# A chunk-selecting attention with an RMS-normed SwiGLU behind it: another recorded engine order, chunk bounds kept as maximum and spread, and the first block's FFN in halves of 128 tokens

## The chip, the cores and the metric

The kernel runs on one core of a Trainium2 chip. Its engines each work through a queue of their own: PE (TensorE, matrix products), DVE (VectorE), ACT (ScalarE), POOL (GpSimd) and SP, which here only starts transfers. The metric is the device time of one execution in microseconds (us); of several executions the median is given.

## The reference

Four sequences of 768 tokens with 8 heads of 64 go through an attention that looks at 6 chunks of 32 keys for each query, and the result goes through a gated FFN:

```python
k_min = np.min(k_chunks, axis=3); k_max = np.max(k_chunks, axis=3)
ub = np.sum(np.maximum(q[:, :, :, None, :] * k_min[:, :, None, :, :],
                       q[:, :, :, None, :] * k_max[:, :, None, :, :]), axis=-1)
ub = np.where(causal, ub, -1e9)
top_chunks = np.argsort(ub, axis=-1)[..., -6:]          # of 24 chunks
scores = np.where(sel & (pos[:, None] >= pos[None, :]), 0.125 * q @ k.T, -1e9)
attn = softmax(scores) @ v                               # (4, 8, 768, 64)
x  = attn.transpose(0, 2, 1, 3).reshape(3072, 512)
xn = x / np.sqrt(np.mean(x * x, -1) + 1e-6) * rms_g
g, val = xn @ w_gate, xn @ w_val                         # 512 -> 1536
out = (g * sigmoid(g) * val) @ w_out                     # 1536 -> 512, float32
```

All inputs are float32 in device memory. `ub` is an upper bound of a query's scores in a chunk.

## The kernel before, in words

The 3072 tokens are cut in 12 blocks of 256 (`ORDER`, line 340): block i is part m of sequence b. For each block and each of its two groups of four heads (`job`, line 605) the work is:

- **Loads** (`load_qk`, `load_v`, lines 423 to 457). k and q come on SP's queue (for block 0 half of them on ACT's, two k loads and two q loads on each, k ahead of q), v and the weights `wg`, `wv`, `wo`, each in three parts, on POOL's. A load of k or q in blocks 0 to 2 ("packed") holds both head groups, later ones hold one.
- **Chunk bounds.** DVE transposes k and q (`turn`, line 628), takes the minimum and maximum of each chunk (`ext0`, `ext1`, line 646) into `kx`, and DVE or POOL forms the spread maximum minus minimum (`dk`, line 652). `bd0` and `bd1` (m = 0) or `KX` (m > 0) spread these into the matrices `BO` and `BD`. With min, and relu(q) (line 725, DVE or POOL), the bound is q·min + relu(q)·(max − min), which PE sums in `upper` (lines 506 to 539).
- **Selection** (`pick`, line 481): DVE turns the bounds (`ubn`), bars a chunk that lies after the query (`bar`), finds the six largest (`top`), compares (`mk`) and turns the mask back (`mt`, `swap`).
- **Attention.** PE multiplies scores and adds the mask times `chunkrow` (lines 751, 762), ACT exponentiates (`exp`, line 801), POOL cuts the triangle (`tri`, line 771), PE multiplies by v with a column of ones (`values`, line 827), DVE divides (`rden`, `norm`, lines 842, 846).
- **Norm** (line 853): a square on ACT, the root on POOL, a scaling (`scale`) on DVE or ACT, a turn on PE (blocks 0 to 3) or by transfers on SP (the others), and for blocks 0 to 3 a multiplication by the gain into `xsT` (line 919).
- **FFN** (line 928): a group is 8 or 16 products with `wg` or `wv` into one of four PSUM buffers `F` (512 columns). Each gate group goes through a tanh on ACT (line 958) and `tg` on DVE (line 962), each value group through a copy on ACT (line 970) and `hh` on POOL (line 973), or `hh` on DVE (line 966). The 12 parts of the hidden layer are then multiplied by `wo` (`project`, line 998), halved into `osb` and stored. In blocks 0 and 1 (`SPLIT`) the first third of the hidden layer is done by 128 tokens at a time (four hidden parts a group, 16 products of 128 columns), so that the FFN can begin when half the block's attention is done; the rest by 256 tokens (two hidden parts a group, 8 products of 256 columns). Either way a group writes 512 columns, and the block has 12 gate and value groups.

What sets the order: nothing is decided at run time. The source calls `plan.op(...)` for each step in program order, and `Plan.run` (line 227) then emits them in the order of the table `STEPS` (lines 47 to 153): a positive entry is 8 times the operation's number plus the engine that does it (steps of `flex`, line 378, can be done by several engines), a negative entry is a run of idle-filling PE products into an `F` buffer (`keep_busy`, line 1063). `SLOTS` (line 156) says which buffer of its pool each step takes. Each engine works through its steps strictly in this order; a step that waits holds up all behind it on its engine. The search that made the table isn't part of the kernel.

The planner's costs beside the operations (for example `0.585, 0.67` in line 646) were used by that search alone; they do nothing when the kernel runs.

Of the kernel before, what the change touches and what calls it, by code (L numbers as in the profile page):

```python
# [8 lines left out]
FP32 = mybir.dt.float32  # L9
BF16 = mybir.dt.bfloat16  # L10
ALU = mybir.AluOpType
# [5 lines left out]
MASKED = -30000.0  # L17
NEG = -1.0e30
HUGE = 3.0e38
# [14 lines left out]
class Plan:  # L34
# [8 lines left out]
    SHARES = ("qx", "scale", "relu", "bd0", "bd1", "dk", "mk")  # L43
# [1053 lines left out]
```

## Time and profile before

| what | value |
|---|---|
| median of 3 runs | 296.39 us (295.38, 296.39, 299.51) |
| the profiled execution's own time | 299.22 us |
| its span, first to last instruction | 297.2 us |
| PE busy | 283.2 us |
| DVE busy | 222.1 us |
| ACT busy | 207.7 us |
| POOL busy | 164.8 us |
| granted TensorE clock, mean | 0.988 |

The profiled execution took 2.0 us more than its span and 2.8 us more than the median. The table counts idle-filling products of line 1066 as busy time of PE, and matmul ends are modelled, so "busy" isn't the same as "useful". The views used below are the page itself, the table of busy time by stretches, the timeline of one engine, groups of instructions by line and shape, the chain that ended last, and the transfers issued in a stretch with their time to landing. Where two times stand at the head of a line of a timeline, they are the start and the duration in us; a bracket gives the idle time before it and what ended it.

### The profile page before, as it was taken

The page shows a single profiled execution, that of the slowest core. Times are in us where ns is not written, and L with a number is a line of the kernel's source. Part 1 is how long each engine was busy: PE and PEld are TensorE (multiplying, and loading weights), DVE is VectorE, ACT ScalarE, POOL GpSimd, SP SyncE. Part 2 cuts the span into 40 slices and gives each one's busy share as a digit, 9 for nine tenths or more (in the row PEclk, how much of TensorE's full clock was granted, in tenths as well). Part 3 has the DMA queues.
Part 4 walks back from the last instruction along what each step waited for, and adds up shares of the span by engine and source line. Part 5 has one row for each costly group of instructions (what it writes and reads, how often), then busy time and mean ns, then how long its engine had stood idle before and what let it go on. Part 6 is the DMA issues. An engine that isn't in the chain of part 4 may idle for free.

```text
span 297.2 us, 11321 instructions
## 1 busy us (share of the span) xinstructions
PE 283.2 (95%) x4667; PEld 214.8 (72%) x4667; DVE 222.1 (75%) x633; ACT 207.7 (70%) x360; POOL 164.8 (55%) x259
## 2 busy tenths in 40 slices
PE   7796998999999999999999999999899999999995
PEld 7544897576867866888776787678668876688773
DVE  4785696899999899998979999978844643447141
ACT  2674786598797986898876797478596777564331
POOL 6985377969889887457593366209141253112510
PEclk9989799999999999999999999999999999999999
DMA  7999996955698877594979455202214001412012
GB/s 188 207 210 207 204 195 114 163 149 65 122 204 145 156 120 117 124 119 103 151 125 152 101 73 99 73 4 73 20 37 109 2 0 37 74 37 71 2 71 71
DMA packets 86387, 31.92 MB, mean 107 GB/s; under 512 B 74817, under 2 KB 81729, under 8 KB 86337
## 3 DMA queue, kind: packets, MB, share of 16 engines
q1 hardware_dynamic: 55776, 22.82, 33.5%
q0 software_dynamic: 29712, 7.87, 26.5%
q8 instruction: 36, 0.59, 0.9%
q10 hardware_dynamic: 848, 0.53, 0.8%
q14 instruction: 15, 0.11, 0.2%
HBM read 28.58 MB, written 6.29 MB: 117 GB/s over the span
## 4 chain that ended last, share of the span: by engine, by line
PE 60%; DVE 19%; DMA 7%; ACT 5%; POOL 4%; issue 3%; ACTq 0%; DVEq 0%
PE F L951 31%; PE F L998 15%; DMA VX<-in_v_dram 6%; PE F L827 5%; PE S L751 4%; DVE kx L646 3%; DVE m L576 2%; DVE tg L962 2%; ACT pt L801 2%; DVE qT L631 2%; PE S L762 2%; DVE mk L582 2%; DVE BD L473 2%; PE F L517 1%; DVE xnat L846 1%
## 5 line engine op out<-in xcount | busy, mean ns | idle before, releaser
L801 ACT ACTIVATE pt<-S 128x1024 bf16<-128x1024 f32 (+3 forms) x104 | 85.6, 861 | 32.7 <-PE S L762 27.6
L973 POOL TENSOR_TENSOR hh<-tg,vs 128x512 bf16<-128x512 bf16 x48 | 56.1, 1176 | 40.2 <-ACT vs L970 20.3
L951 PE MATMUL F<-xsT,wg 128*128 128x256 bf16 (+1 forms) x608 | 73.4, 268 | 1.9 <-DVE xnat L846 0.9
L962 DVE SCALAR_TENSOR_TENSOR tg<-th,F 128x512 bf16<-128x512 bf16 x72 | 48.1, 677 | 35.1 <-ACT th L958 33.8
L951 PE MATMUL F<-xsT,wv 128*128 128x256 bf16 (+1 forms) x608 | 73.3, 269 | 0.9 <-DVE tg L962 0.7
L998 PE MATMUL F<-wo,hh 128*128 128x512 bf16 (+1 forms) x300 | 68.8, 371 | 0.1
L951 PEld LDWEIGHTS <-wg 128*128 128x128 bf16 x608 | 55.6, 98 | 11.5 <-issue 2.3
L951 PEld LDWEIGHTS <-wv 128*128 128x128 bf16 x608 | 55.5, 98 | 10.4 <-issue 1.7
L771 POOL TENSOR_SCALAR_AFFINE_SELECT pt<-pt 128x512 bf16<-128x512 bf16 x48 | 31.9, 671 | 41.2 <-ACT pt L801 41.0
L958 ACT ACTIVATE th<-F 128x512 bf16<-128x512 f32 x72 | 42.7, 604 | 17.2 <-PE F L951 15.8
L998 PEld LDWEIGHTS <-hh 128*128 128x128 bf16 x300 | 27.9, 98 | 26.1 <-issue 1.2
L970 ACT ACTIVATE vs<-F 128x512 bf16<-128x512 f32 x48 | 28.2, 597 | 10.7 <-PE F L951 8.1
L751 PE MATMUL S<-qb,kb 32*128 32x256 bf16 (+1 forms) x800 | 32.8, 254 | 0.4 <-POOL kx L652 0.4
L646 DVE TENSOR_REDUCE kx<-kT 128x16 f32<-128x512 f32 x48 | 30.9, 669 | 0.0
L827 PE MATMUL F<-VX,pt 128*128 128x65 bf16 x672 | 27.5, 195 | 3.0 <-DMA VX<-in_v_dram 2.6
L827 PEld LDWEIGHTS <-pt 128*128 128x128 bf16 x672 | 25.5, 98 | 6.5 <-issue 2.9
L366 POOL DMA_DIRECT2D VX<-in_v_dram x24 | 22.9, 954 | 0.0
L751 PEld LDWEIGHTS <-kb 32*128 32x128 bf16 x800 | 13.6, 93 | 12.8 <-issue 11.4
L762 PE MATMUL S<-mtd,chunkrow 32*128 32x128 bf16 (+2 forms) x384 | 20.4, 204 | 0.0
L762 PE MATMUL S<-mto,chunkrow 32*128 32x128 bf16 (+2 forms) x384 | 19.8, 203 | 0.0
L846 DVE TENSOR_TENSOR xnat<-F,rden 128x256 bf16<-128x256 f32 x48 | 19.2, 412 | 0.7
L762 PEld LDWEIGHTS <-chunkrow 32*128 32x128 bf16 x768 | 18.6, 94 | 0.9
(72 smaller groups left out, 339.9 us busy)
## 6 DMA issues: line engine op xcount, KB each, us to landing
out_dram<-osb SPq DMA_DIRECT2D x23, 256.0 KB, 2.5
kraw<-in_k_dram SPq DMA_DIRECT2D x72, 64.0 KB, 3.1
qraw<-in_q_dram SPq DMA_DIRECT2D x72, 64.0 KB, 3.0
VX<-in_v_dram POOLq DMA_DIRECT2D x24, 128.0 KB, 5.0
QX<-qT SPq DMA_DIRECT2D x32, 64.0 KB, 2.9
wg<-in_moe_w_gate_dram POOLq DMA_DIRECT2D x3, 512.0 KB, 10.0
wv<-in_moe_w_val_dram POOLq DMA_DIRECT2D x3, 512.0 KB, 14.7
wo<-in_moe_w_out_dram POOLq DMA_DIRECT2D x3, 512.0 KB, 17.1
```

Of the source, the lines that this page charges most:

```text
L646: plan.op(f"ext{n}{J}", "DVE", 0.585, 0.67, lambda n=n, op=op: VE.tensor_reduce(out=at(kx)[:, g, n], in_=at(kT).rearrange("p h (j c x) -> ...
L751: TE.matmul(s[a // 2][:, a % 2, c0:c0 + q1 - q0], kbt[r, t, ks], qbt[r, t, q0:q1], start=(t == 0), stop=(t == 1 and not mask), skip_group_ ...
L762: TE.matmul(o, chunkrow[r, BLK * kg + P * e:BLK * kg + P * (e + 1)], mv, start=False, stop=(d == 1), skip_group_check=True)
L771: GE.affine_select(out=d, in_=d, compare_op=ALU.is_ge, fill=0.0, base=0, pattern=[[0, 4], [1, P]], channel_multiplier=-1)
L801: lambda pt=pt, hs=hs, c0=c0, c1=c1, x=sc[hp]: SE.activation(out=at(pt)[:, hs, c0:c1], in_=at(x)[:, :, c0:c1], func=ACT.Exp, scale=SCALE), ...
L827: TE.matmul(o[:, a, :], p_[:, a, off:off + P], vt[:, e, 4 * g + a, :], start=(kb_ == 0 and a == 0), stop=(kb_ == nkb - 1 and a == 3), skip ...
L951: TE.matmul(at(p_)[:, n * W:(n + 1) * W], w[:, g, ht * P:(ht + 1) * P], at(xT)[:, g, x0:x0 + W], start=(g == 0), stop=(g == NP - 1), skip_ ...
L958: plan.op(f"tanh{U}.{hp}", "ACT", 0.48, 0.6, lambda th=th, gp=gp: SE.activation(out=at(th), in_=at(gp), func=ACT.Tanh, scale=0.5), pri - 0 ...
L962: VE.scalar_tensor_tensor(out=at(tg), in0=at(th), scalar=1.0, in1=at(gp), op0=ALU.add, op1=ALU.mult), pri - 30, reads=[th, gp], writes=[tg ...
L970: plan.op(f"vcopy{U}.{hp}", "ACT", 0.48, 0.6, lambda vs=vs, vp=vp: SE.activation(out=at(vs), in_=at(vp), func=ACT.Copy), pri + 0.1, reads= ...
L973: plan.op(f"hh{U}.{hp}", "POOL", 1.11, 1.16, lambda tg=tg, vs=vs, hh=hh: GE.tensor_tensor(out=at(hh), in0=at(tg), in1=at(vs), op=ALU.mult) ...
L998: TE.matmul(at(op)[:, cs], at(key)[:, o:o + P], wo[:, ht, cs], start=(ht == 0), stop=(ht == NHT - 1), skip_group_check=True)
```

## The change

- **Another table.** `STEPS` and `SLOTS` are new throughout, so every engine has another order, and steps with a choice of engine may sit on another one.
- **Bounds.** `kx` now has three planes: minus the minimum (`negate` in the reduction), the maximum, and the spread. The spread is the sum of the first two. Where DVE does it, it is a `tensor_reduce` over the plane axis in place of a `tensor_tensor`; on POOL it stays a `tensor_tensor`. The bound is now q·max + relu(−q)·(max − min), the same number. `relu` can also be done by ACT.
- **FFN.** `CUT` gives the part of the hidden layer that is done by 128 tokens: all of it in block 0, the first third in block 1 as before.
- **Loads.** Block 0's loads can be on SP or ACT each; readiness of k and q is told by head group, so that a turn waits for its own group's loads; `KX` waits no more for k's buffer; `rmsg` isn't tied behind q.
- `chunkrow` can be made by ACT, and the wide filling products read the identity four times over in place of `chunkrow`.

```diff
-    SHARES = ("qx", "scale", "relu", "bd0", "bd1", "dk", "mk")
+    SHARES = ("qx", "scale", "relu", "bd0", "bd1", "mk")
...
-        67, 228, 233, 3, 131, 27, 249, 244, 50, 260, 281, 34, 58, 9, 276, 265, 19, 99, 115, 139,
+        99, 260, 67, 228, 3, 123, 9, 249, 19, 131, 107, 244, 27, 233, 276, 281, 315, 34, 268, 115,
...
-    buffers("kx", 6, [P, NG, 2, 2, CB], FP32)
+    buffers("kx", 6, [P, 3, NG, 2, CB], FP32)
...
+    CUT = {0: NHT, 1: NHT // 3}
...
-        plan.op("chunkrow", "DVE", 0.8, 0.9, lambda: VE.tensor_scalar(
+        def chunks(eng):
+            if eng is SE:
+                return lambda: SE.activation(out=out, in_=x, func=ACT.Copy, scale=MASKED)
+            return lambda: eng.tensor_scalar(out=out, in0=x, scalar1=MASKED, scalar2=None, op0=ALU.mult)
...
-            eng = ("SP", "ACT")[n % 2] if i == 0 else "SP"
...
+                dma(f"load {nm}{b}{m}{a}{k_}", ("SP", "ACT") if i == 0 else ("SP",), sv, dst, packets, cost,
+                    loads_due(i, nm == "q"), writes=[key + (g,) for g in gs],
...
-                axis=AXXY if packed else AXX, op=op), base + 1, ...
+                axis=AXXY if packed else AXX, op=op, negate=not n), base + 1, ...
...
         def sub(eng):
+            if eng is VE:
+                return lambda: VE.tensor_reduce(
+                    out=at(kx)[:, 2, g], in_=at(kx)[:, 0:2, g].rearrange("p n t c -> p t c n"), axis=AXX, op=ALU.add)
             return lambda: eng.tensor_tensor(
-                out=at(kx)[:, g, 1], in0=at(kx)[:, g, 1], in1=at(kx)[:, g, 0], op=ALU.subtract)
+                out=at(kx)[:, 2, g], in0=at(kx)[:, 1, g], in1=at(kx)[:, 0, g], op=ALU.add)
...
-                    reads=[kx_, bd, kraw] + [kx_ + (x, "d") for x in range(NG)], writes=[bd, bd + (m_,)])
+                    reads=[kx_, bd] + [kx_ + (x, "d") for x in range(NG)], writes=[bd, bd + (m_,)])
...
-                eng.tensor_scalar(out=o, in0=x, scalar1=HUGE, scalar2=0.0, op0=ALU.min, op1=ALU.max)
+                if eng is SE:
+                    SE.activation(out=o, in_=x, func=ACT.Relu, scale=-1.0)
+                else:
+                    eng.tensor_scalar(out=o, in0=x, scalar1=-1.0, scalar2=0.0, op0=ALU.mult, op1=ALU.max)
...
-        cut = NHT // 3 if i in SPLIT else 0
+        cut = CUT.get(i, 0)
...
-    plan.ops[-1].after.append([o for o in plan.ops if o.dma and o.name.startswith("load q00")][-1])
...
-            x = chunkrow[:, 0:512] if wide else ident[:]
-            TE.matmul(store["F"][slot][:, 0:x.shape[1]], ident[:], x, start=True, stop=True)
+            n_ = 4 if wide else 1
+            TE.matmul(store["F"][slot][:, 0:n_ * P].rearrange("p (a b) -> p a b", a=n_), ident[:],
+                      ident[:].unsqueeze(1).to_broadcast([P, n_, P]), start=True, stop=True)
```

What the new table says at the places that the prediction speaks of (before, then after):

| engine | before | after |
|---|---|---|
| SP, first | k, k, q, q of block 0 | q, k, k, q, q of block 0 |
| ACT, first | k, k, q, table load, q | table load, k, k, q |
| POOL's transfers, in order | v0 (both halves), wg0, wg1, wv0, wv1, v1 (both halves), wg2, wv2, wo0, wo1, wo2 | wv0, v0 (first half), wg1, v0 (second), v1 (both halves), wg0, wv1, wg2, wv2, wo0, wo2, wo1 |
| PE, filling products: 128 columns, 512 columns | 85, 26 | 71, 28 |
| `dk`: DVE, POOL | 8, 16 | 13, 11 |
| `relu`: DVE, POOL, ACT | 8, 16, 0 | 2, 17, 5 |
| `chunkrow` | DVE | ACT |
| `scale` of block 2, first half | ACT | DVE, behind block 3's selection |

More of the change, by code (lines that the diff above doesn't have):

```diff
@@ L18 @@
 NEG = -1.0e30
-HUGE = 3.0e38
 class Op:
@@ L333 @@
     wo = sb.tile([P, NHT, DM], BF16, name="wo")
-    BD = {b: sb.tile([P, NG, 2, 2, 32], FP32, name=f"BD{b}") for b in range(B)}
+    BD = {b: sb.tile([P, 2, NG, 2, 32], FP32, name=f"BD{b}") for b in range(B)}
     VX = {(b, m): sb.tile([P, 2, H, D + 1], BF16, name=f"VX{b}{m}") for b in range(B) for m in range(NBLK)}
@@ L360, in due_ffn @@
         return PACE * i
-    def dma(name, eng, src, dst, packets, cost, pri, writes, takes=(), reads=(), behind=()):
-        occ = {"SP": 0.49 if pri < -400 else 0.57, "ACT": 0.46, "POOL": 0.78 if packets < 64 else 1.2}[eng]
-        def start():
-            o.inst = issuer[eng].dma_start(out=dst(), in_=src)
-            for p in fences:
-                tc.add_manual_dep(o.inst.ins, p.inst.ins.name, mybir.DependencyInfo(
-                    mybir.DependencyClass.Sync, mybir.DependencyReason.DATA), reason="order")
-        fences = [p for key in behind for p in plan.wrote[key]]
-        o = plan.op(name, eng, occ, occ, start, pri,
-                    reads=list(reads) + list(behind), writes=writes, takes=takes)
-        o.dma = (packets, cost, eng != "POOL")
-        o.slack = MARGIN if pri > -30 and eng == "SP" else 0.0
-        return o
     def flex(name, alts, pri, **kw):
@@ L381, in flex, with dma, start, go @@
         o.alts = alts
+        return o
+    def dma(name, engs, src, dst, packets, cost, pri, writes, takes=(), reads=(), behind=()):
+        engs = (engs,) if isinstance(engs, str) else engs
+        occ = {"SP": 0.57, "ACT": 0.46, "POOL": 0.78 if packets < 64 else 1.2}
+        def start(eng):
+            def go():
+                o.inst = issuer[eng].dma_start(out=dst(), in_=src)
+                for p in fences:
+                    tc.add_manual_dep(o.inst.ins, p.inst.ins.name, mybir.DependencyInfo(
+                        mybir.DependencyClass.Sync, mybir.DependencyReason.DATA), reason="order")
+            return go
+        fences = [p for key in behind for p in plan.wrote[key]]
+        o = flex(name, {e: (occ[e], occ[e], start(e)) for e in engs}, pri,
+                 reads=list(reads) + list(behind), writes=writes, takes=takes)
+        o.dma = (packets, cost, engs[0] != "POOL")
         return o
@@ L403, in constants @@
             -378, reads=["ident"], writes=["pat"])
-        plan.op("chunkrow", "DVE", 0.8, 0.9, lambda: VE.tensor_scalar(
-            out=chunkrow.rearrange("p (c t) -> p c t", t=CH),
-            in0=pat[:, 0:S // CH].unsqueeze(2).to_broadcast([P, S // CH, CH]),
-            scalar1=MASKED, scalar2=None, op0=ALU.mult), -300, reads=["pat"], writes=["chunkrow"])
+        def chunks(eng):
+            out = chunkrow.rearrange("p (c t) -> p c t", t=CH)
+            x = pat[:, 0:S // CH].unsqueeze(2).to_broadcast([P, S // CH, CH])
+            if eng is SE:
+                return lambda: SE.activation(out=out, in_=x, func=ACT.Copy, scale=MASKED)
+            return lambda: eng.tensor_scalar(out=out, in0=x, scalar1=MASKED, scalar2=None, op0=ALU.mult)
+        flex("chunkrow", {"DVE": (2.2, 2.29, chunks(VE)), "ACT": (0.75, 0.84, chunks(SE))}, -300,
+             reads=["pat"], writes=["chunkrow"])
         for i, (key, t) in enumerate(BD.items()):
@@ L426, in load_qk @@
         first = True
-        for n, a in enumerate((0, 2, 1, 3)):
-            eng = ("SP", "ACT")[n % 2] if i == 0 else "SP"
+        for a in (0, 2, 1, 3):
             rows = slice(32 * a, 32 * (a + 1))
@@ L431, in load_qk @@
                 sv = src[b].rearrange("(g a) (m r j) d -> a m r g (j d)", a=4, m=NBLK, r=32)[a, m]
-                todo = [(sv, lambda rows=rows: at(key)[rows].rearrange("r g j h d -> r g (j h d)"),
-                         4, 0.104 if i == 0 else 0.12)]
+                todo = [(sv, lambda rows=rows: at(key)[rows].rearrange("r g j h d -> r g (j h d)"), 4, 0.12, (0, 1))]
             else:
@@ L436, in load_qk @@
                 for g in range(NG):
-                    sv = src[b, 4 * g + a, BLK * m:BLK * (m + 1), :].rearrange(
-                        "(j r) d -> r j d", r=32)
+                    sv = src[b, 4 * g + a, BLK * m:BLK * (m + 1), :].rearrange("(j r) d -> r j d", r=32)
                     todo.append((sv, lambda rows=rows, g=g: at(key)[rows, g].rearrange(
-                        "r j h d -> r j (h d)"), 16, 0.019))
-            for k_, (sv, dst, packets, cost) in enumerate(todo):
-                dma(f"load {nm}{b}{m}{a}{k_}", eng, sv, dst, packets, cost,
-                    loads_due(i, nm == "q"), writes=[key],
-                    takes=[(key, nm + "raw")] if first else (),
+                        "r j h d -> r j (h d)"), 16, 0.019, (g,)))
+            for k_, (sv, dst, packets, cost, gs) in enumerate(todo):
+                dma(f"load {nm}{b}{m}{a}{k_}", ("SP", "ACT") if i == 0 else ("SP",), sv, dst, packets, cost,
+                    loads_due(i, nm == "q"), writes=[key + (g,) for g in gs],
+                    takes=[(key, nm + "raw")] if first else (), reads=() if first else [key],
                     behind=[HELD[i]] if i in HELD and first else ())
@@ L632, in turn @@
                                          in_=at(raw)[:, g]),
-                    base + (0 if nm == "k" else 1) - first, reads=[raw] + ([T] if nm == "q" and g else []),
+                    base + (0 if nm == "k" else 1) - first, reads=[raw, raw + (g,)] + ([T] if nm == "q" and g else []),
                     writes=[T + (g,)], takes=[(T, nm + "T")] if nm == "k" or not g else ())
@@ L646, in job @@
             plan.op(f"ext{n}{J}", "DVE", 0.585, 0.67, lambda n=n, op=op: VE.tensor_reduce(
[L647 removed]
+                out=at(kx)[:, n, g], in_=at(kT).rearrange("p h (j c x) -> p h c j x", j=8, x=4)
                 if packed else at(kT).rearrange("p h (c t) -> p h c t", t=CH),
[L649 removed]
+                axis=AXXY if packed else AXX, op=op, negate=not n), base + 1, reads=[kT, kT + (g,)] + ([kx] if n or g else []), writes=[kx + (g, n)],
                 takes=[(kx, "kx")] if not n and not g else ())
         def sub(eng):
+            if eng is VE:
+                return lambda: VE.tensor_reduce(
+                    out=at(kx)[:, 2, g], in_=at(kx)[:, 0:2, g].rearrange("p n t c -> p t c n"), axis=AXX, op=ALU.add)
             return lambda: eng.tensor_tensor(
[L653 removed]
+                out=at(kx)[:, 2, g], in0=at(kx)[:, 1, g], in1=at(kx)[:, 0, g], op=ALU.add)
         first_dk.append(flex(f"dk{J}", {"POOL": (0.175, 0.22, sub(GE)), "DVE": (0.1, 0.16, sub(VE))},
@@ L657, in place @@
         def place(kx, m):
-            new = BD[b][:, :, :, :, CB * m:CB * (m + 1)].rearrange("p g n t c -> p (g n) t c")
-            old = at(kx).rearrange("p g n t c -> p (g n) t c")
+            new = BD[b][:, :, :, :, CB * m:CB * (m + 1)].rearrange("p n g t c -> p (n g) t c")
+            old = at(kx)[:, 1:3].rearrange("p n g t c -> p (n g) t c")
             copy(new, old)
@@ L730, in job @@
         flex(f"relu{J}", {"POOL": (0.58 if m else 0.25, 0.62 if m else 0.29, relu(GE)),
-                          "DVE": (0.34 if m else 0.14, 0.42 if m else 0.22, relu(VE))},
+                          "DVE": (0.34 if m else 0.14, 0.42 if m else 0.22, relu(VE)),
+                          "ACT": (0.54 if m else 0.24, 0.63 if m else 0.33, relu(SE))},
              base + 2, reads=([qx, qx + (g,)] if m else [qT, qT + (g,)]) + [qraw] + crossed, writes=[qR])
```

6 lines of the change are left out of this document (2 added, 4 removed), and 276 rows, old and new, of tables (SLOTS, STEPS).

## The prediction

> **What bounds the kernel now.** The page is read first, for who is busy; then PE by stage, since a share over the whole span mixes the start with the rest.
>
> ```profile
> PE 283.2 (95%) x4667; PEld 214.8 (72%) x4667; DVE 222.1 (75%) x633; ACT 207.7 (70%) x360; POOL 164.8 (55%) x259
> ...
> PE 60%; DVE 19%; DMA 7%; ACT 5%; POOL 4%; issue 3%; ACTq 0%; DVEq 0%
> ```
>
> PE is busy almost throughout, but only 60% of the chain that ended last is PE; DVE has 19%. The stretches of PE (length, busy time and count, clock, DMA share, GB/s) and, behind them, the filling products of line 1066:
>
> ```profile
> 0.00:30.00 30.00, 23.45 (x415) 0.94 1.24 203
> 30.00:50.00 20.00, 19.20 (x330) 0.91 0.99 177
> 50.00:292.00 242.00, 238.78 (x3925) 1.00 0.52 90
> 0.00:30.00 30.00, 15.31 (x111) 9.56 (x111) 0.94 1.24 203
> ```
>
> In the first 30 us PE idles 6.55 us and fills 15.31 with products that nobody reads: only 8.1 us are work. From 50 us on it idles 242.00 − 238.78 = 3.2 us. So the start has much to give, the rest at most 3.2 us of idle time. But PE isn't alone in the rest. All engines by stretch (columns PE, PEld, DVE, ACT, POOL, then as above):
>
> ```profile
> 23.12:36.35 13.23, 10.32 (x204) 8.33 (x198) 7.64 (x32) 8.59 (x21) 5.36 (x13) 0.87 1.38 201
> 50.00:100.00 50.00, 49.26 (x763) 35.69 (x760) 46.70 (x135) 40.79 (x79) 42.05 (x65) 1.00 0.89 143
> 100.00:165.00 65.00, 64.02 (x1261) 47.75 (x1249) 60.00 (x194) 51.94 (x85) 42.46 (x61) 1.00 0.79 126
> 165.00:210.00 45.00, 43.50 (x862) 34.35 (x859) 41.34 (x130) 34.82 (x57) 22.45 (x32) 1.00 0.39 70
> ```
>
> From 50 to 210 us DVE is busy 46.70 + 60.00 + 41.34 = 148.0 of 160 us (93%): a second bound, so a gain of the start stays only if DVE keeps pace.
>
> **The change part by part.** *The start, up to the first FFN product.* These are the landing of block 0's q on ACT's queue (count, size, median us from issue), DVE's first turn and its step into `xsT`:
>
> ```profile
> qraw<-in_q_dram ACTq DMA_DIRECT2D x2, 128.0 KB, 4.7
> ...
> 4.98 0.71 DVE L631 STREAM_TRANSPOSE kT<-kraw 128x512 f32<-128x512 f32 x1 [2.20 <-DMA kraw<-in_k_dram]
> ...
> 22.23 0.68 DVE L920 TENSOR_TENSOR xsT<-F,rmsg 128x512 bf16<-128x512 bf16 x1
> ```
>
> Before, block 0's k is issued ahead of q, and turned at 4.98. After, q and the table load stand ahead, and the last load of k is the seventh of eight. The eight landed by about 7.0 in the trace (the last was issued at 2.3, and q took 4.7), so k can't be later than 7.0 by much, nor earlier than before: 0 to 2 us late. I take 6.3 (+1.3), near the last landings. Then DVE's queue ahead of `xsT`, by the rows of its operations (count, busy us, mean ns):
>
> ```profile
> L646 DVE TENSOR_REDUCE kx<-kT 128x16 f32<-128x512 f32 x48 | 30.9, 669 | 0.0
> L846 DVE TENSOR_TENSOR xnat<-F,rden 128x256 bf16<-128x256 f32 x48 | 19.2, 412 | 0.7
> L842 DVE RECIPROCAL rden<-F 128x4 f32<-128x4 f32 x48 | 8.0, 172 | 6.4 <-PE F L827 6.2
> L671 DVE TENSOR_TENSOR BO<-kx,own 128x32 f32<-128x32 f32 x6 | 2.7, 444 | 0.5 <-POOL kx L652 0.5
> L560 DVE STREAM_TRANSPOSE ubn<-F 128x32 f32<-128x32 f32 x12 | 1.9, 194 | 3.0 <-PE F L535 3.0
> L473 DVE TENSOR_REDUCE BD<-kx 128x64 f32<-128x64 f32 x12 | 2.5, 206 | 1.1 <-POOL kx L652 1.0
> L404 DVE TENSOR_SCALAR chunkrow<-pat 128x768 bf16<-128x768 bf16 x1 | 0.5, 547 | 0.0
> L725 DVE TENSOR_SCALAR qraw<-qT 128x128 f32<-128x128 f32 x3 | 1.2, 403 | 0.0
> L895 DVE TENSOR_SCALAR xs<-xnat,ri_all 128x512 bf16<-128x512 bf16 x2 | 0.7, 364 | 0.0
> ```
>
> The new order puts ahead of it one more `ext` (0.67), the second `norm` and `rden` of the other token half (0.41 + 0.17), two `bd0` of block 1 (0.89), an `ubn` of two turns (0.39) and a `dk` (0.21, priced as the small reduction of line 473): 2.7 us. It takes away `chunkrow` (0.55), two `relu` (0.81) and a `scale` (0.36): 1.7. Net +1.0. `chunkrow` on ACT falls into PE's filling stretch; without that cover it would cost about its 0.55. So the first FFN product comes 2.3 us later, at 25.4 instead of 23.12.
>
> *From there to the sixth FFN group.* PE's timeline before, with rows left out:
>
> ```profile
> 23.12 1.07 PE L951 MATMUL F<-xsT,wg 128*128 128x128 bf16 x16
> 24.12 0.29 PE L751 MATMUL S<-qb,kb 32*128 32x128 bf16 x8
> 24.34 0.39 PE L1066 MATMUL F<-chunkrow,ident 128*128 128x512 bf16 x1
> 24.66 0.44 PE L535 MATMUL F<-qT,BO 64*64 64x32 f32 x16
> 25.26 1.07 PE L951 MATMUL F<-xsT,wv 128*128 128x128 bf16 x16
> ...
> 29.63 0.29 PE L827 MATMUL F<-VX,pt 128*128 128x65 bf16 x4 [2.42 <-DMA VX<-in_v_dram]
> 30.42 1.66 PE L951 MATMUL F<-xsT,wg 128*128 128x256 bf16 x8
> ...
> 33.58 0.64 PE L827 MATMUL F<-VX,pt 128*128 128x65 bf16 x8
> ...
> 34.58 1.05 PE L951 MATMUL F<-xsT,wg 128*128 128x256 bf16 x8
> 35.46 1.06 PE L951 MATMUL F<-xsT,wv 128*128 128x128 bf16 x16
> 36.35 1.06 PE L951 MATMUL F<-xsT,wg 128*128 128x128 bf16 x16
> ```
>
> Six groups are through at 36.35, 13.2 us after the first began. A group takes 0.88 at full speed (34.58 to 35.46). The 13.2 are: 6 × 0.88 = 5.3; idle 13.23 − 10.32 = 2.9, of which 2.42 waits for block 1's v; the two groups from 30.42 to 33.58, 3.16 instead of 1.76, so 1.4 lost right behind that wait, where the clock of the stretch is 0.87; one fill, 0.3; attention, the remaining 3.3.
>
> That v was issued behind four weight parts:
>
> ```profile
> 12.22 1.82 POOL L366 DMA_DIRECT2D VX<-in_v_dram  x2
> VX<-in_v_dram POOLq DMA_DIRECT2D x1, 128.0 KB, 17.3
> 19.48 1.04 PE L1066 MATMUL F<-chunkrow,ident 128*128 128x512 bf16 x4
> ```
>
> It landed at 12.2 + 17.3 = 29.5. After, two weight parts stand ahead of it, so it lands some us earlier while its `values` comes later: I count the 2.9 of idle and the 1.4 as gone. Next late is the weights: wg0, wv1 and both v are together with what was before the first six transfers, thus in by about 13.1 + 17.3 = 30.4; wv1 is wanted behind the fifth group, near 32. Of the attention, one `scores` (0.22) and one `upper` (0.60) go ahead of the first group, into the time that it waits; a fill of four (1.04) comes into the stretch. So 25.4 + 5.3 + 1.0 + (3.3 − 0.8) = 34.2 against 36.35: **2.1 us gained**. The bounds are 3.4 (k no later) and 0 (the waits come back, below).
>
> *The middle.* `dk` on DVE, and the place where it hurt:
>
> ```profile
> L652 DVE TENSOR_TENSOR kx<-kx 128x16 f32<-128x16 f32 x8 | 3.9, 493 | 0.0
> 70.19 1.88 DVE L652 TENSOR_TENSOR kx<-kx 128x16 f32<-128x16 f32 x2
> 75.51 1.03 PE L951 MATMUL F<-xsT,wv 128*128 128x256 bf16 x8 [0.71 <-DVE tg L962]
> ```
>
> As a reduction, 13 × 0.21 = 2.7 replaces 3.9; six `relu` less save 6 × 0.40 = 2.4; `chunkrow` 0.5: DVE has 4.1 us less. The five `relu` on ACT go to an engine that is 70% busy. PE gets of this at most its 3.2 us of idle time, at least nothing (or a loss, below). I take 0.7: the one wait (75.51) that stands behind the stretched pair of `dk`.
>
> *The halves* give 8 groups of 16 products where 8 products stood: 0.89 against 0.88 us (35.46 to 36.35, 34.58 to 35.46), 0.1 in all. `negate`, the third plane, the readiness by head group and the identity as filler issue no instruction more; between nothing and 0.1 us each, taken as nothing.
>
> Sum: −2.1 − 0.7 + 0.1 = −2.7, from 299.2 to 296.5 for an execution like the profiled one. That one lies 2.8 above the median of 296.39, so the forecast is **293.7 us**.
>
> **The rivals.** *More than that.* If k lands no later, the start gives 3.4, and if DVE's relief reaches PE whole, 3.2: 296.4 − 6.5 = 289.9. For it speaks that DVE is 93% busy where the chain runs over it; against it, that PE's waits there are spread over many small ones. Chance 0.17.
>
> *A wait takes the place of the one removed.* The queue carries the same bytes, at about 200 GB/s through the whole start (203 and 177 above). If PE comes to wg2 or wv2 before they land, or DVE doesn't keep pace, it waits the 2.1 us there: 296 to 299 with the later start. Chance 0.20. In here lies that the reductions are stretched too, which alone costs 0.7.
>
> *Each 128-column product paced by its weight load.*
>
> ```profile
> L951 PEld LDWEIGHTS <-wg 128*128 128x128 bf16 x608 | 55.6, 98 | 11.5 <-issue 2.3
> ```
>
> At 98 ns for each, block 0's 128 products that replace 64 would take 12.5 us instead of 64 × 0.11 = 7.0: 5.5 more, 299.2. Against it stands 0.89 us for 16 products, 56 ns each. Chance 0.02. The Trainium skill's page "TensorE: Matmul & The Clock Gate", section "Back-to-back issue gap", speaks for it: it gives 81 ns as the sustained spacing of 128-column products with their weight loads. By that figure the halves would cost an estimated 3.4 us and the kernel would come to 297.0; the trace, at 56 ns, disagrees with it for this stream.
>
> *Slower: DVE's order.* In block 2 the `scale` ahead of PE's turn moves from ACT to DVE, behind block 3's whole selection, and PE's strict queue waits for it, as for every `tg`. If DVE's busy share from 50 to 210 falls from 93% to 88%, its 148.0 − 4.1 = 143.9 us take 163.5 instead of 160, and PE loses 3.5; at 85%, 169.3 and 9.3. With the start's gain gone into the same wait, that is 300 to 305.7, 303 in the middle. It decides where DVE's share falls under 90%, since 143.9 / 0.9 = 160. For it speaks the high share; against it, that DVE has less to do. Chance 0.11.
>
> **How the numbers follow.** Forecast 0.50 with a range of its own of 291.5 to 296; 0.17 for 289.9; 0.22 for 296 to 299; 0.11 for about 303. What a measurement of this kernel can tell from no change is about 2%, 5.9 us: faster is under 290.5, slower over 302.3. The faster rival lies mostly under it: 0.15; of the slower one about two thirds lie over it, 0.08; the same 0.77. The range for 8 in 10 goes from 289.5 to 300.5: it takes in the forecast, the waits that come back and most of the faster rival.
>
> **What would show it.** Right: no wait of PE for VX over 0.5 us; first product with `wg` or `wv` at 25 ± 1 us; six groups through by 34 to 35; DVE's `kx` reduction near 0.2 us, without one over 1 us; DVE busy from 50 to 210 about 4 us less in sum. Wrong: a first FFN product behind 27 us, a wait of PE for `wg` or `wv` between 28 and 45 us, 128-column groups over 1 us apart, or PE idle over 6 us between 50 us and its end.

## The result: slower, 308.21 us, and what the profile after shows

The changed kernel takes 308.21 us (median of 6, 307.25 to 311.38); the kernel before took 297.81 us beside it (6 runs, 295.38 to 299.71). The ratio is 1.0365 with a 95% interval of 1.0293 to 1.0437. The forecast was 293.7 us, and the range ended at 300.5. Ratios here leave out executions that lie over 1.5% above the fastest of the same kernel (in the runs below three of eleven in e6, its profiled one among them, two of ten in e9, one of twelve in e11), so they can differ a little from the quotient of two medians.

The profiled execution took 309.2 us, with a span of 307.0. From the page of the changed kernel, the busy time of each engine and the chain by engine:

```profile
PE 284.2 (93%) x4719; PEld 215.7 (70%) x4719; DVE 221.1 (72%) x626; ACT 211.8 (69%) x366; POOL 187.0 (61%) x257
...
PE 64%; DVE 11%; DMA 9%; POOL 8%; issue 3%; ACT 2%; SPq 2%; DVEq 0%; POOLq 0%; ACTq 0%
```

PE has as much work as before (284.2 against 283.2). POOL has 22 us more (187.0 against 164.8) and twice the share of the chain. The stretches, first of PE alone, then of PE, PEld, DVE, ACT and POOL (busy time and count), each with clock, DMA share and GB/s behind it:

```profile
0.00:30.00 30.00, 23.26 (x477) 1.00 1.24 216
30.00:50.00 20.00, 19.49 (x380) 1.00 1.01 162
50.00:302.00 252.00, 240.72 (x3879) 0.99 0.48 86
...
50.00:100.00 50.00, 46.29 (x662) 33.02 (x660) 42.77 (x119) 40.79 (x80) 40.33 (x56) 1.00 0.83 139
100.00:165.00 65.00, 59.15 (x1102) 44.84 (x1109) 53.38 (x156) 48.72 (x80) 47.68 (x59) 0.95 0.64 105
165.00:210.00 45.00, 44.27 (x924) 32.71 (x914) 40.73 (x142) 32.76 (x54) 28.04 (x36) 1.00 0.49 89
```

Up to 50 us nothing is lost. From 50 us on PE idles 252.00 − 240.72 = 11.3 us where it idled 3.2. DVE isn't fuller but emptier: 42.77 + 53.38 + 40.73 = 136.9 us from 50 to 210, against 148.0. It waits too. PE's timeline of the start, the first two FFN groups and the sixth:

```profile
24.98 1.07 PE L962 MATMUL F<-xsT,wg 128*128 128x128 bf16 x16
25.89 1.06 PE L962 MATMUL F<-xsT,wv 128*128 128x128 bf16 x16
...
32.90 1.06 PE L962 MATMUL F<-xsT,wv 128*128 128x128 bf16 x16
33.80 0.42 PE L838 MATMUL F<-VX,pt 128*128 128x65 bf16 x8
```

The first FFN product comes at 24.98 and six groups are through at 33.80, 2.5 us earlier than before. So the start went as forecast, and the loss lies behind it. PE's longest waits (in all, times, longest) name a cause:

```profile
PE F L521 <- POOL qraw L735: 7.7, 5, 3.6
PE F L1076 <- POOL ident masks.py:199: 3.3, 1, 3.3
PE F L539 <- DVE BO L678: 2.5, 4, 1.4
```

`qraw` written by POOL at line 735 is the relu, which stood in no wait of PE before. The groups of that line in the changed kernel, and the `dk` reductions of DVE (count, busy us, mean ns):

```profile
L735 POOL TENSOR_SCALAR qraw<-QX 128x512 f32<-128x512 f32 x14 | 26.9, 1928 | 6.7 <-DMA QX<-qT 6.6
L735 POOL TENSOR_SCALAR qraw<-qT 128x128 f32<-128x128 f32 x3 | 2.3, 759 | 0.1
L657 DVE TENSOR_REDUCE kx<-kx 128x16 f32<-128x32 f32 x13 | 2.2, 172 | 0.1
```

and of the relu on POOL in the kernel before:

```profile
L725 POOL TENSOR_SCALAR qraw<-QX 128x512 f32<-128x512 f32 x11 | 6.8, 623 | 5.9 <-DMA QX<-qT 5.8
L725 POOL TENSOR_SCALAR qraw<-qT 128x128 f32<-128x128 f32 x5 | 1.8, 362 | 0.7 <-DVE qT L631 0.7
```

The same 128x512 float32 operation went from 0.62 to 1.93 us. It costs POOL 14 × (1.928 − 0.623) + 3 × (0.759 − 0.362) = 19.5 us. The worst place, in the changed kernel's timelines of POOL, PE and DVE:

```profile
127.61 3.81 POOL L735 TENSOR_SCALAR qraw<-QX 128x512 f32<-128x512 f32 x2 [5.43 <-DMA QX<-qT]
...
131.47 0.68 PE L521 MATMUL F<-qraw,BD 64*32 64x128 f32 x16 [3.58 <-POOL qraw L735]
...
133.09 0.78 DVE L564 STREAM_TRANSPOSE ubn<-F 128x256 f32<-128x256 f32 x2 [6.00 <-PE F L521]
133.80 5.21 DVE L892 SCALAR_TENSOR_TENSOR xs<-xnat,ri_all,gB 128x512 bf16<-128x512 bf16 x2
```

POOL's two relus end 3.81 us after their `QX` landed, PE waits 3.58 us for them, DVE waits 6.00 for PE. Then comes a second thing: DVE's two `xs` take 5.21 us together.

### The profile page after: what moved, and what is told of

Read it like the earlier page. It is cut to its first block, busy times and chain, and to the rows that moved or that the text cites. A ratio compares the mean times of both kernels' runs of the same rounds, so it can differ in the third digit from the quotient of the medians.

```text
span 307.0 us, 11434 instructions
## 1 busy us (share of the span) xinstructions
PE 284.2 (93%) x4719; PEld 215.7 (70%) x4719; DVE 221.1 (72%) x626; ACT 211.8 (69%) x366; POOL 187.0 (61%) x257
## 4 chain that ended last, share of the span: by engine, by line
PE 64%; DVE 11%; DMA 9%; POOL 8%; issue 3%; ACT 2%; SPq 2%; DVEq 0%; POOLq 0%; ACTq 0%
PE F L962 31%; PE F L1009 16%; PE F L838 5%; PE S L762 5%; POOL qraw L735 5%; DMA xsT<-xs 3%; DVE xs L892 3%; DMA qraw<-in_q_dram 2%; DMA kraw<-in_k_dram 2%; PE S L773 2%; DMA QX<-qT 2%; PE F L521 2%; POOL hh L984 1%; DVE tg L973 1%; SPq L375 1%
## 5 line engine op out<-in xcount | busy, mean ns | idle before, releaser
L962 PEld LDWEIGHTS <-wv 128*128 128x128 bf16 x640 | 56.4, 98 | 11.0 <-issue 1.6
L962 PEld LDWEIGHTS <-wg 128*128 128x128 bf16 x640 | 56.8, 99 | 9.5 <-issue 0.2
L762 PE MATMUL S<-qb,kb 32*128 32x256 bf16 (+1 forms) x800 | 33.5, 255 | 1.0 <-issue 0.5
L735 POOL TENSOR_SCALAR qraw<-QX 128x512 f32<-128x512 f32 x14 | 26.9, 1928 | 6.7 <-DMA QX<-qT 6.6
L977 DVE TENSOR_TENSOR hh<-tg,F 128x512 bf16<-128x512 bf16 x24 | 16.4, 682 | 14.4 <-PE F L962 13.9
```

The costliest lines, as they stand in the source:

```text
L735: eng.tensor_scalar(out=o, in0=x, scalar1=-1.0, scalar2=0.0, op0=ALU.mult, op1=ALU.max)
L762: TE.matmul(s[a // 2][:, a % 2, c0:c0 + q1 - q0], kbt[r, t, ks], qbt[r, t, q0:q1], start=(t == 0), stop=(t == 1 and not mask), skip_group_ ...
L962: TE.matmul(at(p_)[:, n * W:(n + 1) * W], w[:, g, ht * P:(ht + 1) * P], at(xT)[:, g, x0:x0 + W], start=(g == 0), stop=(g == NP - 1), skip_ ...
```

## The experiments

Two theories stood first. **The relu**: its new form (multiply by −1, then maximum with 0) is slow on POOL, and PE waits for it. **The order**: the new table puts steps where they are late, whatever their form. In all runs the kernel before ran on the same chip beside them; its medians were 298.04 (first four), 298.05 (the next four), 297.40 (e9, e10) and 298.58 (e11).

### One part at a time

`e1_new_order_minmax`, the changed kernel with the old form of the relu on POOL and DVE. It leaves out the relu's sign, so other chunks are chosen; the steps and their sizes stay the same:

```diff
-                    eng.tensor_scalar(out=o, in0=x, scalar1=-1.0, scalar2=0.0, op0=ALU.mult, op1=ALU.max)
+                    eng.tensor_scalar(out=o, in0=x, scalar1=3.0e38, scalar2=0.0, op0=ALU.min, op1=ALU.max)
```

> The changed kernel, but relu on POOL and DVE is min with 3e38, then max with 0, as it was before, in place of times -1, then max with 0 (the sign is left out, so the bounds of those steps are others). Theory A (the form of relu on POOL costs the time: 14 steps of 1.93 us instead of about 0.62, PE waits 7.7 us for them): the wide relu on POOL falls to about 0.62 us, PE's waits for it to under 1 us, and the time to 296 to 300 us. Theory B (the new order itself is worse behind the start, and POOL's longer steps only show where it waits): still 304 us or more. Theory C (both): between.

Measured: 300.47 us (300.05 to 304.18), ratio 1.0127 (1.0044 to 1.021). The form alone takes 308.21 − 300.47 = 7.7 us, which is as much as PE waited for the relu (7.7), and in e1's profile no wait of PE for the relu is left. But 1.3% remains.

`e2_old_order_multmax`, the reverse: the kernel before with the new form (the rest of the bound is left as it was, so other chunks are chosen here too).

```diff
-                eng.tensor_scalar(out=o, in0=x, scalar1=HUGE, scalar2=0.0, op0=ALU.min, op1=ALU.max)
+                eng.tensor_scalar(out=o, in0=x, scalar1=-1.0, scalar2=0.0, op0=ALU.mult, op1=ALU.max)
```

> The kernel before with the new form of relu alone (times -1, then max with 0, on POOL and DVE; the rest of the bound is not changed with it, so the bounds are others). Theory A: the 11 wide relu on POOL take 1.9 us each, 14 us more POOL time, PE waits for several of them, 302 to 308 us. Theory B: PE's waits stay small and the time is that of before, 296 to 299 us.

Measured: 307.0 us (304.66 to 307.27), ratio 1.0298 (1.0216 to 1.0381). That one line costs the old kernel 9.0 us. Its group of relus:

```profile
L725 POOL TENSOR_SCALAR qraw<-QX 128x512 f32<-128x512 f32 x11 | 21.5, 1954 | 5.7 <-DMA QX<-qT 5.6
```

`e3_new_order_old_bounds`: the new table, loads and halves, with the old bounds (minimum, and spread by subtraction) and the old relu.

```diff
-    buffers("kx", 6, [P, 3, NG, 2, CB], FP32)
+    buffers("kx", 6, [P, NG, 2, 2, CB], FP32)
...
-            if eng is VE:
-                return lambda: VE.tensor_reduce(
...
-                    SE.activation(out=o, in_=x, func=ACT.Relu, scale=-1.0)
+                    SE.activation(out=o, in_=x, func=ACT.Relu, scale=1.0)
...
-                    eng.tensor_scalar(out=o, in0=x, scalar1=-1.0, scalar2=0.0, op0=ALU.mult, op1=ALU.max)
+                    eng.tensor_scalar(out=o, in0=x, scalar1=3.0e38, scalar2=0.0, op0=ALU.min, op1=ALU.max)
```

> The changed kernel's order, loads and FFN halves with all of the old bounds: minimum and spread, spread by a tensor_tensor on DVE too, relu as min and max, ACT's relu without the sign. Theory A: as e1 or up to 1.5 us slower, 296 to 301 us, since only the 13 spreads on DVE cost more (0.5 instead of 0.2 us each). Theory B: 304 us or more. If this one is over 2 us slower than e1, the small reduction is worth more than the 0.7 us that were forecast.

Measured: 301.83 us (299.97 to 303.31), ratio 1.0142 (1.0062 to 1.0221). So the order, with its loads and halves, is slower by about 1.4%, although in its profile the sixth FFN group begins at 34.44 us, 1.0 us earlier than in the kernel before (35.46).

`e4_old_order_new_spread`: the old table with the third plane, `negate` and the reduction, and the old relu.

```diff
-    buffers("kx", 6, [P, NG, 2, 2, CB], FP32)
+    buffers("kx", 6, [P, 3, NG, 2, CB], FP32)
...
+            if eng is VE:
+                return lambda: VE.tensor_reduce(
+                    out=at(kx)[:, 2, g], in_=at(kx)[:, 0:2, g].rearrange("p n t c -> p t c n"), axis=AXX, op=ALU.add)
```

> The kernel before with the three planes, the negated minimum and the spread by reduction on DVE, relu still as min and max (so without its sign; the bounds are others). Forecast in the prediction: 0.7 us less than before, at most 3.2, at least nothing: 295 to 298 us; the stretched pair of spreads (1.88 us) near 0.4. If negate or the reduction are slow in themselves: the reductions of the chunk bounds over 0.7 us or the spread over 0.4 us, and 299 us or more.

Measured: 298.14 us (295.37 to 299.07), ratio 0.9995 (0.9956 to 1.0034). The reduction does what it is for (0.17 us each, none stretched) and gives the end nothing that can be measured.

So both theories hold: against the kernel before, the relu is about three quarters of the loss (7.7 of 10.4 us), the order the rest.

### Which forms are slow on POOL

`e5_relu_seven_forms`, the changed kernel with POOL's relus cycling over seven forms:

```diff
-                    eng.tensor_scalar(out=o, in0=x, scalar1=-1.0, scalar2=0.0, op0=ALU.mult, op1=ALU.max)
+                    f = len(tried) % 7
+                    tried.append(f)
+                    if f == 0:
+                        eng.tensor_scalar(out=o, in0=x, scalar1=-1.0, scalar2=0.0, op0=ALU.mult, op1=ALU.max)
...
```

> The changed kernel, in which POOL's 17 relus take seven forms in turn: (0) mult by -1 then max with 0, (1) min with 3e38 then max with 0, (2) min with 0 then mult by -1, (3) mult by -1 alone, (4) max with 0 alone, (5) mult by -1 then add 0, (6) add 0 then max with 0. Forms 1, 3, 4, 5 and 6 leave out the sign or the clamp, so the chunks that they choose are others; the work behind them is the same. What is measured is the duration of one 128x512 relu of each form on POOL: 1.92 us in the changed kernel, 0.61 us with the old form. If every arithmetic operation on POOL is slow: 0, 2, 3, 5 and 6 at 1.2 us or more, 1 and 4 at 0.6. If only mult is: 0, 2, 3 and 5 slow, 6 at 0.6. If only a mixed pair (an arithmetic operation and a comparison) is slow: 0, 2 and 6 at 1.9, 1, 3, 4 and 5 at 0.6. If the slow part is a negative scalar with mult: 0, 2, 3, 5 slow, and nothing tells it from mult alone.

The one execution took 302.57 us. The groups by line, one line for each form. In the order of the rows: add then max (753), min then mult (745), mult then max (741), mult alone (747), max alone (749), mult then add (751), min then max (743).

```profile
L753 POOL TENSOR_SCALAR qraw<-QX 128x512 f32<-128x512 f32 x2 | 3.9, 1954 | 0.4 <-DMA QX<-qT 0.4
L745 POOL TENSOR_SCALAR qraw<-QX 128x512 f32<-128x512 f32 x2 | 3.9, 1936 | 4.9 <-DMA QX<-qT 4.8
L741 POOL TENSOR_SCALAR qraw<-QX 128x512 f32<-128x512 f32 x2 | 3.8, 1923 | 0.5 <-issue 0.5
L747 POOL TENSOR_SCALAR qraw<-QX 128x512 f32<-128x512 f32 x2 | 3.0, 1520 | 0.0
L749 POOL TENSOR_SCALAR qraw<-QX 128x512 f32<-128x512 f32 x2 | 3.0, 1506 | 0.0
L751 POOL TENSOR_SCALAR qraw<-QX 128x512 f32<-128x512 f32 x2 | 1.3, 632 | 0.1
L743 POOL TENSOR_SCALAR qraw<-QX 128x512 f32<-128x512 f32 x2 | 1.2, 610 | 0.7 <-DMA QX<-qT 0.7
```

It isn't the multiplication: multiply then add takes 0.63 us. A pair of two arithmetic operations or of two comparisons is fast (0.63, 0.61), a mixed pair takes 1.92 to 1.95 us in either order, which is what the third outcome foretold for the pairs. It missed for one operation alone, which takes 1.5 us instead of 0.6: leaving out the second operation makes it slower, not faster. Why is open.

### What the order loses

In e3 PE idles 240 − 231.29 = 8.7 us between 50 and 290 us, before 240 − 236.78 = 3.2. The timelines of e3 at the two places where most of it lies, first DVE, POOL and PE near 60 us, then DVE, POOL, SP and PE from 125:

```profile
59.80 2.42 DVE L732 TENSOR_SCALAR qraw<-qT 128x128 f32<-128x128 f32 x1
...
59.86 2.27 POOL L981 TENSOR_TENSOR hh<-tg,vs 128x512 bf16<-128x512 bf16 x2
...
62.38 0.43 PE L539 MATMUL F<-qT,BO 64*64 64x32 f32 x16 [1.48 <-DVE BO L675]
...
125.93 4.60 DVE L889 SCALAR_TENSOR_TENSOR xs<-xnat,ri_all,gB 128x512 bf16<-128x512 bf16 x2
...
126.07 0.62 POOL L643 CAST qb<-qT 128x512 bf16<-128x512 f32 x1
...
128.90 1.06 POOL L691 COPY QX<-qT 128x512 f32<-128x512 f32 x1
...
130.91 2.55 SPq L895 DMA_TRANSPOSE xsT<-xs  x2
...
138.14 1.86 PE L959 MATMUL F<-xsT,wv 128*128 128x256 bf16 x8 [2.88 <-DMA xsT<-xs]
```

Both show one pattern: a DVE step on operands in SBUF starts beside POOL steps that stand back to back, and is held. The relu ends at 62.22, with POOL's two `hh` (62.13). Of the two `xs` the first takes 3.57 us, while POOL does four steps; POOL's next one, the copy at 128.90 (0.60 us in e6), then takes 1.06. In the kernel before POOL was idle beside the same two `xs`, and they took 0.74 and 0.71 us:

```profile
127.85 0.74 DVE L881 SCALAR_TENSOR_TENSOR xs<-xnat,ri_all,gB 128x512 bf16<-128x512 bf16 x1
...
129.13 0.71 DVE L881 SCALAR_TENSOR_TENSOR xs<-xnat,ri_all,gB 128x512 bf16<-128x512 bf16 x1
...
129.78 1.16 POOL L771 TENSOR_SCALAR_AFFINE_SELECT pt<-pt 128x512 bf16<-128x512 bf16 x1 [3.33 <-ACT pt L801]
```

The Trainium skill's page "SBUF — State Buffer", section "🔬 SBUF: two separate sides", states such a thing: a DVE operation with two SBUF inputs (against a GpSimd operation that reads SBUF), or in a mode that takes both ports, and the GpSimd operation exclude each other, and the loser blocks until the other is through. The traces agree (0.7 us against 3.57 for the first `xs`).

Three runs test it. `e6_pool_waits_for_xs` adds one wait to e3: POOL's `half q` (5051) starts when both `xs` (4130, 4114) are done.

```diff
-        5202, 6980, 9752, 4537, 5051, 5580,
+        5202, 6980, 9752, 4537, 4130, 4114, 5051, 5580,
...
-            pool = lambda: GE.tensor_copy(natural(at(hb)), order(turned(nm)))
+            def pool():
+                o = GE.tensor_copy(natural(at(hb)), order(turned(nm)))
+                if nm == "q" and J == (2, 1, 0):
+                    tc.add_manual_dep(o.ins, weighed[5, 0].ins.name, mybir.DependencyInfo(
+                        mybir.DependencyClass.Sync, mybir.DependencyReason.DATA), reason="order")
+                return o
```

> The new order with the old bounds and the old relu (301.83 us) with one wait added: the POOL step 'half q' behind block 5's norm, and with it everything queued on POOL after it, starts when both of DVE's xs of that block are done. Nothing else differs. If DVE's xs is held by POOL's back-to-back steps: the two xs take 0.7 to 0.75 us each instead of 4.60 together, xsT lands about 3 us earlier, PE's wait of 2.9 us for xsT and the lower clock behind it go, and the time is 298 to 299.5. If the transposes or SP's queue set the landing: xs is short and the wait stays, 301 to 302. If POOL's steps, 1 to 2 us later, are late for someone in turn: the wait moves to a tile that POOL writes (qb, hh, pt), 300.5 to 302.

Measured: 298.51 us (296.67 to 304.35), ratio 0.9997 (0.9955 to 1.004). The profiled execution was the longest of the eleven. Its timelines of DVE, POOL, SP and PE:

```profile
125.94 1.38 DVE L759 SCALAR_TENSOR_TENSOR xs<-xnat,ri_all,gB 128x512 bf16<-128x512 bf16 x2
...
127.39 0.61 POOL L508 CAST qb<-qT 128x512 bf16<-128x512 f32 x1 [1.30 <-DVE xs L759]
...
126.85 2.28 SPq L239 DMA_DIRECT2D qraw<-in_q_dram  x1
...
130.72 2.55 SPq L766 DMA_TRANSPOSE xsT<-xs  x2
...
138.03 1.86 PE L830 MATMUL F<-xsT,wv 128*128 128x256 bf16 x8 [3.85 <-DMA xsT<-xs]
```

A wait that makes POOL stand idle for 1.3 us takes 4.60 us down to 1.38: the collision is shown. It repeats: without the wait the two `xs` take 4.61 us in e7 too, with it 1.37 in e8, e9 and e10. The median is 3.3 us lower than e3's. How much of that is the collision's isn't shown, because e3's four executions lie apart (299.97, 300.42 and 303.24, 303.31), and in its profile the FFN starts later: the sixth group begins at 34.44, in e6's at 32.34. The second outcome came true as well in the profiled execution: SP issues the transposes only at 130.72, behind a load that holds it for 2.28 us, and PE waits as long as ever. In e8's profile, too, they come 2.9 us behind their `xs` (128.14 against 125.25). That may be why the times of this kernel scatter; no run shows it.

`e7_relu_on_act` moves the relu of 59.80 from DVE to ACT, and `e8_both` joins it with e6's wait.

```diff
-        2812, 1994, 2884, 2506, 2128, 2466, 2475,
+        2812, 1994, 2884, 2505, 2128, 2466, 2475,
```

> The new order with the old bounds and the old relu (301.83 us) with one step moved: the relu of 128x128 that took 2.42 us on DVE at 59.80, beside two hh of POOL, is done by ACT, which stood idle there. If that stretched relu costs what PE waits behind it (1.48 us for BO): 300.3 to 301. If the next step is late anyway (BO's other inputs, the chunk bits): 301.5 to 302.

> Both edits of the two runs before it. If DVE steps held by POOL are what is left of the slowdown: 296.5 to 298.5, no slower than the kernel before, because the start's 2 us are then kept. If the two gains are eaten by one and the same later wait: 298.5 to 300.5. If neither edit touches the cause: 301.5 to 302.

Measured: e7 302.65 us (300.76 to 303.64), ratio 1.0145 (1.0082 to 1.0208), no gain over e3; e8 299.77 us (297.21 to 301.14), ratio 1.0042 (1.0006 to 1.0078), no gain over e6. In e7's profile the FFN starts late, at 28.34 us, so its time alone can't tell what the move is worth. The timelines of DVE, POOL and PE in e8 show what came in its place:

```profile
57.71 2.39 DVE L544 TENSOR_TENSOR BO<-kx,own 128x32 f32<-128x32 f32 x1
...
57.78 2.27 POOL L852 TENSOR_TENSOR hh<-tg,vs 128x512 bf16<-128x512 bf16 x2
...
60.16 0.43 PE L403 MATMUL F<-qT,BO 64*64 64x32 f32 x16 [1.34 <-DVE BO L544]
```

The relu is gone, and the next DVE step, the small `BO` on two SBUF inputs that PE waits for, is held by the same two `hh` (2.39 us; 2.40 in e7). A held step that goes makes room for the next one.

`e9_transposes_ahead` is e6 with the two transposes ahead of the four loads on SP's queue (`across50` and `across51`, 4124 and 4140, stand with both scales ahead of `load q2200`, 6980). `e10_all_held_steps` is e8 with that move and with the held `BO` (2466) on POOL, ahead of the `hh`. Both changes, as e10 has them:

```diff
-        2812, 1994, 2884, 2505, 2128, 2466, 2475,
+        2812, 1994, 2884, 2505, 2128, 2467, 2475,
...
-        5202, 6980, 9752, 4537, 4130, 4114, 5051, 5580,
+        5202, 4130, 4114, 4124, 4140, 6980, 9752, 4537, 5051, 5580,
```

> As e6_pool_waits_for_xs (298.51 us), and block 5's two transposes stand on SP's queue ahead of the four loads that held them in that run: there both xs were done at 127.32 and the transposes were issued at 130.72, behind a load of 2.28 us and three more. If SP's queue is the second half of the cause: the transposes are issued within 0.3 us of their xs, PE's wait for xsT (3.9 us in that profile) falls under 0.5, and the time is 296 to 298 with less spread. If the landing is slow by itself (the transposes' own time in the DMA queues): issue early, the wait stays over 1 us, 298 to 299. If the four loads, 2 to 3 us later, are late for DVE's turns: the wait goes to qT, kT or S, 298 to 300.

> As e9_transposes_ahead, with the relu on ACT (e7) and the BO step that took its place under POOL's two hh (2.39 us on DVE at 57.71 in e8_both) done by POOL ahead of them. If DVE's steps held by POOL and the transposes behind SP's loads are all that the new order lost: no BO wait over 0.4 us at 60, PE idle between 50 us and the end at 4 us or less (8.7 in e3), and 294.5 to 296.5, faster than the kernel before by 0.5 to 1%. If each stall that goes lets the next one show: 296.5 to 299. If the order's loss lies elsewhere: as e8_both, 299 to 300.

Measured: e9 298.65 us (297.09 to 302.0), ratio 1.0016 (0.998 to 1.0052); e10 296.61 us (294.83 to 299.16), ratio 0.9989 (0.9951 to 1.0028). The timelines of SP, DVE and PE in e9:

```profile
126.17 2.54 SPq L766 DMA_TRANSPOSE xsT<-xs  x2
...
131.71 0.71 DVE L499 STREAM_TRANSPOSE kT<-kraw 128x512 f32<-128x512 f32 x1 [1.63 <-DMA kraw<-in_k_dram]
...
133.05 1.03 PE L830 MATMUL F<-xsT,wv 128*128 128x256 bf16 x8 [0.85 <-DVE hh L845]
```

and of e10, its stretch from 50 us, its two FFN rows of the start, and its waits for `BO` and `chunkrow`:

```profile
50.00:290.00 240.00, 235.01 (x3854) 1.00 0.50 90
...
24.59 1.07 PE L830 MATMUL F<-xsT,wg 128*128 128x128 bf16 x16
...
32.61 1.06 PE L830 MATMUL F<-xsT,wv 128*128 128x128 bf16 x16
...
PE F L403 <- DVE BO L544: 1.6, 4, 0.6
PE S L639 <- ACT chunkrow L274: 1.3, 1, 1.3
```

In e9 the transposes are issued 0.8 us behind their `xs` (done at 125.34; 0.3 was expected) and the wait for `xsT` is gone from the profile, yet the median isn't better than e6's: the first outcome missed. The trace shows the third one. The loads now stand behind the transposes, DVE waits 1.63 us for k at 131.71, its `hh` behind that comes late, and PE waits 0.85 us for it. With these held steps taken out, e10 is 301.83 − 296.61 = 5.2 us faster than e3 (4.6 by the two ratios), and PE idles 5.0 us from 50 to 290 instead of 8.7. No wait for `BO` is left near 60 us; those shown lie in the start. But 4 us of idle time or less was expected for the first outcome, and the time lies just inside the second: each stall that goes lets another show. The new order is then as fast as the old one, not faster.

`e11_chunkrow_early` is e10 with the two steps that make `chunkrow` (50 and 57) at the front of their engines.

```diff
-        315, 34, 268, 115,
+        315, 34, 50, 57, 268, 115,
```

> As e10_all_held_steps (296.61 us), and the two steps that make chunkrow stand first on their engines: the reduction of ident (DVE, 0.32 us at 14.51 there) behind own at 3.4 us, where DVE then stands idle until 5.87, and the copy on ACT (0.84 us at 15.11) behind its loads, where ACT stands idle until 6.62. PE's wait of 1.26 us for chunkrow at 16.01 goes. If PE's order sets the end from there on: 295.2 to 295.8, faster than the kernel before by 0.5 to 0.9%. If the start is paced by the loads of k and q behind it (the first FFN products wait for those in any case): 296.3 to 296.9, as e10.

Measured: 297.30 us (294.63 to 301.32), ratio 0.9975 (0.9938 to 1.0011). PE no longer waits for `chunkrow`; it waits 0.81 us at 17.52 for the mask instead. The time lies just over the second outcome's range. The interval holds no change, so no version here is shown to beat the kernel before.

| kernel | median us | ratio to the kernel before |
|---|---|---|
| the changed kernel | 308.21 | 1.0365 (1.0293 to 1.0437) |
| e1: old relu | 300.47 | 1.0127 (1.0044 to 1.021) |
| e3: old relu, old bounds | 301.83 | 1.0142 (1.0062 to 1.0221) |
| e6: and POOL waits for `xs` | 298.51 | 0.9997 (0.9955 to 1.004) |
| e10: and transposes ahead, relu on ACT, `BO` on POOL | 296.61 | 0.9989 (0.9951 to 1.0028) |

## Why the prediction was wrong

- **The start: right.** 25.4 was forecast for the first FFN product, 24.98 came; 34.2 for six groups, 33.80 came. k's first turn came at 5.74, not 6.3; from there to `xsT` the time grew by the 1.0 us that was forecast, though by 1.5 more of work on DVE and 0.5 less of waiting, so there the sum was lucky. PE's wait for `VX` and the slow products behind it are gone (the clock of the first 30 us is 1.00 instead of 0.94). A half group takes 0.91 us from start to start, so the rival of the weight loads at 98 ns each falls.
- **The middle: this step failed.** It counted the relu only where it moved between engines, "six `relu` less" on DVE and five more on ACT, and left POOL's share at its old duration without a word. The diff shows another pair of operations, and no row of before shows that pair on POOL, so its cost was unknown and needed a bound, as the small parts beside it were given one. Even the price of another POOL step on 128x512, `hh` at 1.18 us, would have put 14 × 0.56 = 8 us on an engine that others wait for; the step really rose from 0.62 to 1.93, 18 us for the 14. The term was worth 7.7 us on the new order and 9.0 on the old one.
- **The sum: the start's gain was carried to the end whole.** This failed too. With the old relu, e1 is still 6.8 us over the forecast. The start's part of the sum, 2.0 us with the halves, would be a ratio of 0.993; e10, with the old relu, the old bounds and the held steps taken out, has 0.9989 (0.9951 to 1.0028). The order's stalls behind 50 us stood in the sum at nothing, and in e3 they are 8.7 − 3.2 = 5.5 us of PE's idle time. The gain was also read from a single profiled execution, and its 2.5 us were measured between one on each side. The sixth group begins at 35.46, 35.16 and 33.55 us in the three profiles with the old table (before, e2, e4), and between 31.92 (e11) and 35.74 (e7) in the ten with the new one. The middle values are 2.5 us apart, but the ranges overlap. What takes this gain in e10, which idles only 1.8 us more than the kernel before from 50 to 290, is not settled.
- **`dk`: right in size, nothing in effect.** 13 reductions take 2.2 us (2.7 forecast) and none is stretched. In e4 the pair that took 1.88 us takes 0.28, beside the same three POOL steps, and the ratio is 0.9995. Whether PE gained the 0.7 us can't be told: that would be 0.9977, inside e4's interval.
- **DVE's relief: wrong in what it means.** DVE was busy 11.1 us less from 50 to 210, not 4.1, and that was the mark of a slower kernel: it stood waiting. Over the whole span its busy time fell by 1.0 us (222.1 to 221.1). A busy time that falls is a gain only if PE's idle time doesn't grow.
- **The slower rival: its condition came true, its mechanism didn't.** DVE's share fell to 136.9 / 160 = 86%, and that rival was said to decide under 90%. But no wait of PE for the `scale` that had moved to DVE stands in the profile, and about half of the fall is the relu's: with its old form, in e1, the share is 142.4 / 160 = 89%. What the order did cost (e3: 3.8 us over the kernel before) came at least in part from DVE steps that now start beside POOL's back-to-back ones. The row that could have shown it was quoted: the two `kx` steps at 70.19 that took 1.88 us together, a step of 0.2 us elsewhere, while POOL did three steps back to back (70.18 to 71.94). It was read as a fault of that step, which the change mends, and not as something that can befall any DVE step at such a place.
- **The marks that were named:** those for right that concern the start and the `kx` reduction came true in a slower kernel; none of them looks at POOL, or at PE's waits behind 50 us. Of those for wrong, one told: "PE idle over 6 us between 50 us and its end"; it was 11.3.

## What to carry to other kernels

When a diff rewrites an operation's two ALU functions, treat it as a new operation on each engine that does it, and look for its price on the slowest of them before anything else. When an order changes, look not only at how full each engine is but at which of DVE's steps with SBUF operands will start beside a run of POOL steps; a wait that made POOL idle for 1.3 us took 3.2 us off two held steps here. After taking out one held step, look at the next one on the same engine before counting the gain.

## What the hardware did that was not expected

- POOL's `tensor_scalar` on 128x512 float32 takes 0.61 to 0.63 us with a pair of like operations (two comparisons, two arithmetic), 1.92 to 1.95 us with a mixed pair and 1.5 us with one operation alone. On 128x128 it is 0.40 against 0.76 us.
- A DVE step that meets POOL steps back to back can be held through several of them: `BO` of 128x32, 0.28 us on average in e10, took 2.39 us in e8 and ended with the second of two `hh` (60.10 and 60.05); the first `xs` in e3 took 3.57 us, through four POOL steps.
- Beginning first did not help the held step. By the records DVE's had begun before POOL's each time: 59.80 against 59.86 and 125.93 against 126.07 in e3, 57.71 against 57.78 in e8.
